# A decode-attention kernel whose loads of K, V and weights go through one ring of 4 MiB contiguous tiles

## The chip, the cores and the metric

The kernel runs on one core of a Trainium2 chip. The metric is device time in microseconds (us), the median of several executions. Before the change it is 2669.64 us (three runs, 2669.05 to 2670.12). Timed experiments come with a 95% interval from fast runs alone. An experiment of a single look has one time beside a run of the kernel before on the same chip; its state is unknown, and I use it only for differences far above 1%, or together with its trace.

## The reference, cut to what matters

```python
x  = A_x                                    # 1 x 1 x 448, bf16
xn = layernorm(x)
q  = (xn @ wq) -> 16 heads x 256            # wq 448 x 4096
scores = q . k_cache * 256**-0.5            # k_cache 16 x 65536 x 256, bf16 (537 MB)
o  = softmax(scores) @ v_cache              # v_cache the same size
s  = o.reshape(4096) @ wo                   # wo 4096 x 448
g  = silu(silu(xn @ w1) @ w2)               # w1 448 x 1792, w2 1792 x 448
out = x + s * g
```

One query token attends to 65536 cached tokens in 16 heads. Every byte of K and V is used once, so the kernel is a reader of 1074 MB with some arithmetic beside it.

One weakness of this reference: s·g is tiny beside x. So the comparison doesn't prove the attention of any kernel here; it is right by construction where the same sums are made.

## The kernel before

K comes in units of 2 MiB (128 partitions x 32 rows of 256). VectorE makes 19 of the 32 dot products of a partition with one fused instruction each, and a wide product for the other 13, which ScalarE sums one by one. (Each fused instruction and each sum stands in before's trace as two, the second reading the total out: 417 and 80 ns on the mean on DVE, 401 and 186 on ACT. So the counts below are about twice those of the loops.)

```python
kp_pool = tc.tile_pool(name="kp", bufs=3);  v_pool = tc.tile_pool(name="vp", bufs=4)
...
Kh = K_t[0, h].rearrange("(j c) d -> j c d", j=P)          # a partition's rows: 256 KiB apart
k_eng.dma_start(out=Kp[:, :, :], in_=Kh[:, kd * KC : (kd + 1) * KC, :])
for i in range(ND):                                          # ND = 19
    nc.vector.tensor_tensor_reduce(out=junk[:, :], in0=Kp[:, i, :], in1=qh, ...,
                                   op0=ALU.mult, op1=ALU.add, accum_out=S_d[:, u, i : i + 1])
nc.vector.tensor_tensor(out=prod[:, :, :], in0=Kp[:, ND:KC, :], in1=qh broadcast, op=ALU.mult)
for i in range(NPU):                                         # NPU = 13
    nc.scalar.activation(out=junk2[:, :], in_=prod[:, i, :], func=ACT.Identity,
                         accum_out=S_a[:, u, i : i + 1])
```

After 8 such units (a block, half a head) a softmax over the block follows. Then TensorE (PE) multiplies the weights with V, 32 matmuls of 256 columns per 2 MiB of V, while the K units of the next block are interleaved. K and V loads share one queue (q1 in the page), issued by SyncE (SP) in the order of the program. wq, w1, w2 and wo are loaded first, and the whole query and the MLP are computed before the first K load, issued at 59.4 us, since the K buffers lie where those weights lay.

## Time and profile before

| what | before |
|---|---|
| time | 2669.64 us |
| DMA, share of its 16 engines' time | over 90% in slices 3 to 39 of 40 |
| VectorE (DVE) busy | 2229.9 us, 84%, 10312 instructions |
| ScalarE (ACT) busy | 1397.5 us, 52%, 6843 instructions |
| PE busy | 1469.9 us, 55%, 8722 matmuls and 8722 weight loads |

The page cuts the span into 40 equal slices; a digit is the busy share in tenths, and the row "GB/s" is what the 16 DMA engines moved together. The prediction shows those rows. A part of the page that it did not show becomes the centre of this case, so here it is, the page's part 3 for before (queue, kind: packets, MB, share of the time of 16 engines):

```profile
q8 instruction: 68, 1.11, 0.2%
q14 instruction: 145, 1.19, 0.1%
```

The page calls their kind "instruction", and their number follows that of the instructions: 10240 more on DVE bring 79 more packets on q14 (e2 below), 17408 more PE records bring 68 on q8 (e3). So I read them as the engines' own programs, fetched while they run. They cost the DMA engines that bring K and V time, as the packet records below show (975 ns for one). The sizes follow from the lines: 1.19 MB / 145 is 8 KiB on q14, 1.11 MB / 68 is 16 KiB on q8, and those packets have 8192 and 16384 B in the trace. The counts of e2 and e3 make 130 instructions to a packet of q14 and 256 to one of q8. With 128, my rounding, DVE's 10312 make 81 and ACT's 6843 make 53 packets, which with about 8 that do not belong to the loops (the experiment e1 below has 8 with almost no instructions) gives 142 of the 145 on q14. PE's 17444 records at 256 to a packet make 68, which is q8. In the share column this is nothing: 0.1% and 0.2%.

### The profile page before, as it was taken

To read this page: it belongs to the slowest core of one execution; us is meant where nothing else is said; L and a number is where in the kernel's file an instruction comes from. 1 tells how busy PE (TensorE), PEld (TensorE's weight loads), DVE (VectorE), ACT (ScalarE), POOL (GpSimd) and SP (SyncE) were. 2 spreads that over 40 slices of the span, in tenths; PEclk is the share of its full clock that TensorE was granted. 3 is DMA by queue.
4 is the path that set the end of the run, shared out by engine and by line. 5 is a ranking of instruction groups with operands and counts; after the bars stand their busy time and mean duration, and the time that the engine had idled before them with its cause. 6 is when DMAs were issued, how large, how long until landed. Compare 5 with 4: busy or idle time off the path is not lost.

```text
span 2669.2 us, 36113 instructions
## 1 busy us (share of the span) xinstructions
PE 1469.9 (55%) x8722; PEld 912.7 (34%) x8722; DVE 2229.9 (84%) x10312; ACT 1397.5 (52%) x6843; POOL 1.6 (0%) x12
## 2 busy tenths in 40 slices
PE   4055655555556565555555555555555565555556
PEld 2033333333333333333333333333333333333334
DVE  1998888888888888888888888888888888888983
ACT  0565555555555555545555554555555555555552
POOL 0000000000000000000000000000000000000000
PEclk9577777777776877777787777677777767776778
DMA  5899999999999999999999999999999999999996
GB/s 197 336 416 427 427 427 427 427 424 414 416 415 419 424 414 412 417 411 417 427 412 419 409 414 422 422 412 417 411 418 426 413 415 413 419 411 425 413 420 279
DMA packets 80919, 1086.63 MB, mean 407 GB/s; under 512 B 8385, under 2 KB 14274, under 8 KB 14722
## 3 DMA queue, kind: packets, MB, share of 16 engines
q1 hardware_dynamic: 74242, 1077.45, 95.9%
q10 hardware_dynamic: 6432, 6.88, 0.8%
q8 instruction: 68, 1.11, 0.2%
q14 instruction: 145, 1.19, 0.1%
q0 software_dynamic: 32, 0.00, 0.0%
HBM read 1084.29 MB, written 0.00 MB: 406 GB/s over the span
## 4 chain that ended last, share of the span: by engine, by line
DMA 48%; DVE 42%; ACT 6%; PE 2%; issue 1%; ACTq 0%; DVEq 0%; SPq 0%
DMA Kp<-in_A_k_cache_dram 46%; DVE junk L258 31%; DVE prod L271 9%; ACT junk L279 6%; DMA Vt<-in_A_v_cache_dram 1%; PE ps_O L426 1%; DMA wo_sb<-in_A_wo_dram 1%; DVE S_d L258 1%; PE ps_q L166 0%; DVE gm L305 0%; DVE rmax_a L298 0%; PE ps_y L216 0%; PE ps_h L203 0%; DVE dlt L357 0%; DVE q_row_bf L188 0%
## 5 line engine op out<-in xcount | busy, mean ns | idle before, releaser
L279 ACT ACTIVATE junk<-prod 128x256 bf16<-128x256 bf16 x3328 | 1330.7, 401 | 1129.2 <-DVE prod L271 1078.8
L258 DVE CUSTOM_DVE_ANT_0 junk<-Kp,qb 128x256 bf16<-128x256 bf16 x4864 | 1709.2, 417 | 251.1 <-DMA Kp<-in_A_k_cache_dram 249.9
L426 PE MATMUL ps_O<-Vt,P_V 128*1 128x256 bf16 x8192 | 1404.0, 353 | 927.0 <-DMA Vt<-in_A_v_cache_dram 927.0
L426 PEld LDWEIGHTS <-P_V 128*1 128x1 bf16 x8192 | 875.8, 107 | 1445.7 <-issue 967.7
L279 ACT ACTIVATION_READ_ACCUMULATOR junk<-prod 128x1 f32 x3328 | 620.6, 186 | 0.0
L271 DVE TENSOR_TENSOR prod<-Kp,qb 128x3328 bf16<-128x3328 bf16 x256 | 482.2, 1884 | 0.0
L258 DVE DVE_READ_ACCUMULATOR2_ANT S_d<- 128x1 f32 x4864 | 387.8, 80 | 0.0
L301 PE MATMUL ps_mrow<-ident_bf,rmax 128*1 128x128 bf16 x32 | 7.9, 247 | 180.4 <-DVE rmax L299 180.4
L301 PEld LDWEIGHTS <-rmax 128*1 128x1 bf16 x32 | 2.5, 79 | 192.4 <-DVE rmax L299 192.4
L298 DVE TENSOR_REDUCE rmax_a<-S_a 128x1 bf16<-128x104 f32 x32 | 8.5, 264 | 59.1 <-ACT junk L279 59.1
L386 DVE SCALAR_TENSOR_TENSOR o_row<-ps_O,cf,o_row 1x256 f32<-1x256 f32 x16 | 7.5, 472 | 60.0 <-PE ps_O L426 60.0
L311 ACT ACTIVATE negb<-ps_nb 128x1 f32<-128x1 f32 x32 | 5.5, 171 | 51.4 <-PE ps_nb L307 51.4
L324 PE MATMUL ps_tot<-ones_col_f,rsum_d 128*1 128x1 f32 x64 | 6.1, 164 | 27.1 <-ACT P_V L315 27.1
L324 PEld LDWEIGHTS ps_tot<-ones_col_f,rsum_d 128*1 128x1 f32 x64 | 2.7, 81 | 43.5 <-ACT P_V L315 43.5
L152 PE MATMUL ps_gen_i<-one_bf,xn_bf 1*128 1x1 bf16 (+1 forms) x4 | 0.4, 178 | 28.0 <-DVE xn_bf L142 28.0
L140 DVE RECIPROCAL rstd<-rstd 1x1 f32<-1x1 f32 x1 | 0.2, 151 | 18.1 <-ACT rstd L137 18.1
L137 ACT ACT_TABLE_LOAD x1 | 1.3, 1283 | 25.6 <-issue 25.6
L396 PE MATMUL ps_ot<-one_f,o_row 1*128 1x1 f32 x64 | 9.6, 251 | 9.0 <-DVE o_row L386 9.0
L315 ACT ACTIVATE P_V<-S_d,negb 128x152 bf16<-128x152 f32 x32 | 13.6, 424 | 1.0
L396 PEld LDWEIGHTS ps_ot<-one_f,o_row 1*128 1x128 f32 x64 | 8.3, 185 | 13.7 <-DVE o_row L386 13.7
L198 ACT CAST qb<-ps_qb 128x512 bf16<-128x512 f32 x5 | 2.9, 586 | 18.6 <-PE ps_qb L191 18.6
L403 DVE CAST OT<-ps_ot 128x2 bf16<-128x2 f32 x16 | 2.6, 160 | 11.1 <-PE ps_ot L396 11.1
(60 smaller groups left out, 167.5 us busy)
## 6 DMA issues: line engine op xcount, KB each, us to landing
Kp<-in_A_k_cache_dram SPq DMA_DIRECT2D x256, 2048.0 KB, 21.7
Vt<-in_A_v_cache_dram SPq DMA_DIRECT2D x256, 2048.0 KB, 26.1
wo_sb<-in_A_wo_dram ACTq DMA_DIRECT2D x1, 3584.0 KB, 23.6
wq_sb<-in_A_wq_dram SPq DMA_DIRECT2D x3, 1024.0 KB, 8.3
w_sb<-in_B_w_dram ACTq DMA_DIRECT2D x1, 1568.0 KB, 8.6
w_sb<-in_B_w_dram ACTq DMA_DIRECT2D x3, 448.0 KB, 8.5
wq_sb<-in_A_wq_dram SPq DMA_DIRECT2D x1, 512.0 KB, 13.9
w_sb<-in_B_w_dram ACTq DMA_DIRECT2D x1, 224.0 KB, 5.3
```

The source lines that it names most:

```text
L198: nc.any.tensor_copy(out=qb[:, g * 512 : (g + 1) * 512], in_=ps_qb[:, :])
L258: nc.vector.tensor_tensor_reduce(out=junk[:, :], in0=Kp[:, i, :], in1=qh, scale=1.0, scalar=0.0, op0=ALU.mult, op1=ALU.add, accum_out=S_d[ ...
L271: nc.vector.tensor_tensor(out=prod[:, :, :], in0=Kp[:, ND:KC, :], in1=qh[:, None, :].to_broadcast([P, NPU, Dh]), op=ALU.mult,)
L279: nc.scalar.activation(out=junk2[:, :], in_=prod[:, i, :], func=ACT.Identity, accum_out=S_a[:, u, i : i + 1],)
L298: nc.vector.reduce_max(out=rmax_a[:, :], in_=S_a[:, :, :], axis=AX.XY)
L301: nc.tensor.matmul(ps_mrow[0:1, :], lhsT=rmax[:, 0:1], rhs=ident_bf[:, :], start=True, stop=True)
L311: nc.scalar.mul(out=negb[:, :], in_=ps_nb[:, :], mul=-scale)
L315: nc.scalar.activation(out=P_V3[:, :, 0:ND], in_=S_d[:, :, :], func=ACT.Exp, bias=negb[:, 0:1], scale=scale, accum_out=rsum_d[:, 0:1],)
L324: nc.tensor.matmul(ps_tot[0:1, 0:1], lhsT=rsum_d[:, 0:1], rhs=ones_col_f[:, 0:1], start=True, stop=(S_a is None),)
L386: nc.vector.scalar_tensor_tensor(out=o_row[0:1, :], in0=ps_O[0:1, :], scalar=cf[0:1, b : b + 1], in1=o_row[0:1, :], op0=ALU.mult, op1=ALU.add,
L396: nc.tensor.matmul(ps_ot[:, n : n + 1], lhsT=o_row[0:1, a * P : (a + 1) * P], rhs=one_f[0:1, 0:1], start=True, stop=True,)
L426: nc.tensor.matmul(ps_O[0:1, :], lhsT=P_V[:, cvl : cvl + 1], rhs=Vt[:, i, :], start=(cvl == 0), stop=(cvl == CPB - 1),)
```

## The change

The intent: keep the DMA engines fed from the first microsecond to the last.

- One ring of five 4 MiB tiles serves wq, K, V and the last weights; every tile is one contiguous stretch of memory, 32 KiB per partition.
- Loads are issued in a fixed order: wq, K, K, then K and V by turns, V a softmax block behind K; w1, w2 and wo come behind the last V.
- The query is computed on all partitions directly, one group of 512 columns at once, so that K work starts after the first group.
- A fixed program order: products ahead of dots, so that ScalarE sums beside DVE; the softmax spread over later half tiles; a block is 16384 tokens.
- V matmuls take two tokens at a time: 512 columns instead of 256.

```diff
-N_DVE_PER_UNIT = 19
-NUM_BLOCKS = 2
+KT = 64
+SUB = 32
+ND = 19
+TPB = 2
+RING = 5
...
+    ring = ctx.enter_context(tc.tile_pool(name="ring", bufs=RING))
+    ctx.enter_context(tc.manual_schedule())
...
+    nc.sync.dma_start(
+        out=wq_t[0:DP, 0 : DC * HD], in_=A_wq.rearrange("(p c) n -> p (c n)", c=DC)
+    )
+    Kh = A_k_cache[0].rearrange("h (t p c) d -> h t p (c d)", p=P, c=KT)
+    Vh = A_v_cache[0].rearrange("h (t p c) d -> h t p (c d)", p=P, c=KT)
...
+    for ki, (h, t) in enumerate(tiles):
+        Kt = load_k(h, t)
+        for s in range(NS):
+            prod = products(h, Kt, s)
+            turn()
+            sums(h, t, s, prod)
+            dots(h, t, Kt, s)
+        if vi < (ki // TPB) * TPB:
+            vh, vt = tiles[vi]
+            attend(vh, vt, load_v(vh, vt))
...
+        if t % TPB == TPB - 1:
+            block_max(h, t // TPB)
+    while vi < len(tiles):
+        vh, vt = tiles[vi]
+        Vt = load_v(vh, vt)
+        if vi == len(tiles) - 1:
+            ... loads of w1, w2 and wo into ring tiles
```

The dots and the sums themselves stay what they were: 19 fused instructions and 13 sums per 32 rows.

## The prediction

> **What bounds the kernel now.** I read the page's slices first, then a table of windows, the queue's own waits, and the chain and timeline of the end. The slices:
>
> ```profile
> PEclk9577777777776877777787777677777767776778
> DVE  1998888888888888888888888888888888888983
> ...
> DMA  5899999999999999999999999999999999999996
> GB/s 197 336 416 427 427 427 427 427 424 414 416 415 419 424 414 412 417 411 417 427 412 419 409 414 422 422 412 417 411 418 426 413 415 413 419 411 425 413 420 279
> ```
>
> The DMA engines are full from slice 3 to slice 39, at 427 GB/s on the best plateau. 1073.7 MB of K and V (16 heads x 65536 x 256 x 2 bytes, twice) must be read whatever the program is. VectorE (DVE) at 8 tenths is second. So the bound is the transfer, and the question is where the 16 engines do not run at 427. The windows answer (columns: window, length, busy of PE, weight load, DVE, ACT, POOL with instruction counts, granted clock, DMA share, GB/s):
>
> ```profile
> 0.00:66.70 66.70, 27.38 (x242) 17.81 (x242) 9.95 (x22) 6.50 (x10) 1.57 (x12) 0.96 0.57 197
> 66.70:133.50 66.80, 0.00 (x0) 0.00 (x0) 66.22 (x312) 37.05 (x182) 0.00 (x0) 0.50 0.83 336
> 200.00:500.00 300.00, 165.34 (x981) 102.67 (x980) 258.84 (x1203) 163.15 (x802) 0.00 (x0) 0.76 1.01 427
> 1000.00:1500.00 500.00, 279.40 (x1629) 172.33 (x1626) 427.73 (x1985) 269.37 (x1326) 0.00 (x0) 0.75 0.99 417
> 2600.00:2640.00 40.00, 25.40 (x167) 16.44 (x166) 22.34 (x98) 17.02 (x84) 0.00 (x0) 0.74 0.76 305
> 2640.00:2670.00 30.00, 22.22 (x197) 16.37 (x194) 1.85 (x4) 0.00 (x0) 0.00 (x0) 0.98 0.59 250
> ```
>
> Time lost against 427 is length x (1 - rate/427). Head (0 to 200 us, with the stretch of 133.5 to 200 at 416): 35.9 + 14.2 + 1.7 = 51.8 us. Middle (200 to 2600; 418, 417, 415 and 416 in the four windows of 500 us, 423 in the last 100): 10.5 + 11.7 + 14.1 + 12.9 + 0.9 = 50.1 us. Tail: 11.4 + 12.4 = 23.8 us. Sum 125.7; and 1086.63 MB / 427 = 2544.8 us, which with 125.7 makes 2670 us. The account closes.
>
> The **head**: the queue has nothing to move while the query and the MLP are computed.
>
> ```profile
> 36.00:40.00 4.00, 3.37 (x40) 2.89 (x39) 1.36 (x3) 0.00 (x0) 0.00 (x0) 1.00 0.00 0
> ...
> SPq L254 <- DVE g_f L225: 25.7, 1, 25.7
> ```
>
> The first K load waits 25.7 us for the gate g_f, since the K buffers lie where the init weights lay. Then three 2 MiB K buffers, with no V allowed before the first softmax, leave the rate at 336 while DVE works.
>
> The **middle**: the queue is in order, and stops where a K buffer is not yet free.
>
> ```profile
> 1008.76 0.33 SPq L254 DMA_DIRECT2D Kp<-in_A_k_cache_dram  x1
> 1009.18 0.38 SPq L423 DMA_DIRECT2D Vt<-in_A_v_cache_dram  x1
> 1022.19 0.33 SPq L254 DMA_DIRECT2D Kp<-in_A_k_cache_dram  x1
> ...
> 1020.00:1024.00 4.00, 2.00 (x19) 1.41 (x17) 3.96 (x16) 1.80 (x9) 0.00 (x0) 1.00 0.57 197
> ...
> DVE rmax_a L298 <- ACT junk L279: 59.1, 30, 5.2
> ```
>
> Loads are normally 8 to 10 us apart, but once per softmax block the gap is 13.4 us: DVE waits for ScalarE's last sums (59.1 us in 30 waits), K comes free late, V stands behind K, and the engines run dry for about 2 us. The early plateau at 427 does not contradict this: the K issues recur at the same 80 to 81 us per block throughout, so the early blocks were living on V transfers queued during the head.
>
> The **tail**: the last K lands at 2614.8; the last V tiles wait for the last softmax and for four V buffers; the last V lands at 2659.9 and 9.3 us of finishing follow.
>
> [...]
>
> **The change part by part.**
>
> *Work on the engines.* DVE's K work is the same per 2 MiB: 19 dots at a pitch of 345 ns (6.56 us) and one product of 1.82 us, 8.4 us. Per 4 MiB tile it is 16.8, and one K plus one V tile take 8.39 MB / 427 = 19.65 us. A block of two tiles is then 33.6 + about 1.5 of softmax = 35 of 39.3 us. The products now come before the dots, so ScalarE's 13 sums (5.3 us) run under the 6.56 us of dots and the rmax_a wait goes. V: 4096 matmuls of 512 columns instead of 8192 of 256, the same streamed columns[...]. PE fits.
>
> *Buffers.* The ring holds five 4 MiB tiles, shared. In steady state K lands at time 0 and is used up by about 20; its slot is next written at 39.3. V lands[...], and is rewritten after 39. V lags by a block: P·V's weights are ready about 21 us after the block's last K lands, while the first V of that block lands 29.5 us after it. A new stall exists: the maximum's small matmul stands in PE's order behind a V tile[...], and slots have 20 us of slack. So the middle loss goes from 50.1 to about 0.
>
> *Head.* wq (3.67 MB) and then K are issued at once; query(0) needs only wq. DVE starts slower than the transfer (K at 21, 31, 41 us; done at 33, 50, 70), and I checked each slot in order: wq's slot is free near 27 and wanted at 51; the first K's at 33, wanted at 60; the third K's at 70, wanted at 80; the fourth K's at 87, wanted at 100. None stalls. Left: 2.3 us before bytes flow (183 GB/s in the first 4 us of before) and about 1.1 us for wq at 380 instead of 427 (the rate of before's weight loads): 3.4 instead of 51.8 us.
>
> *Tail.* MLP and out weights (6.88 MB, about 18.1 us at 380, of which 16.1 are in the byte sum) follow the last V. Work after the last V byte, from before's durations: [...]32 matmuls at 0.22, 7.0; copy of the block 0.7; 16 fp32 turns recorded as 32 at 0.15, 4.8; hidden layer 4.1 (56 recorded in 4.07); silu in four small ops 1.0; ps_y 4 (14 in 4.74[...]); 32 out matmuls of 448 columns 8.5[...]; two 0.61 us ops and a store of 2.4, 3.7. Sum 35.8 us after the last V byte, so 35.8 - 16.1 = 19.7 us are loss (before: 23.8). The tail gains little: the final work moves onto the path while weights load under part of it.
>
> *Sum.* 2544.8 + 3.4 + 0 + 19.7 = 2568. Less about 1 us of instruction fetch (some 8000 fewer PE records of 36113; 2.3 MB of fetch in all)[...]: **2563 us**, 4% less than 2669.6.
>
> **The rivals.** (a) *The transfer itself changes rate.* [...]If the true sustainable rate is about 418 and early 427 was special, 54 us more: 2617. Against it: full windows between dips in the middle still read 426. (b) *DVE becomes the bound* through fixed order: the max wait behind V, or a write conflict on the one score tile that ScalarE and DVE now share (before kept two). [...]If dots had to wait for ScalarE's sums on every half tile, 8.4 + 5.3 = 13.7 us x 256 half tiles = some 3500 us. The instructions write disjoint columns, so I hold this unlikely. (c) *The head is not gained*: a late query or a slot not free in the first blocks; at most 30 us back, 2593. (d) *The tail grows*[...].
>
> **Range and chances.** Most of the gain is arithmetic of idle DMA time seen in the trace: 48 head, 50 middle, 4 tail. Rivals (a), (c), (d) move it by 10 to 40 us. Range 2538 to 2608. The 2% line is 2616; only a full (a) or (b) crosses it. Faster 0.93, same 0.05, slower 0.02.
>
> **What would show it.** Right: GB/s near 427 from slice 1 to 39 with no dips; DVE about as busy (2200 us) but waiting for K and not holding it; queue waits short of starving; the first dot near 16 us; DMA idle only in the last 18 us. Wrong: a DMA share of 1.0 at a rate under 420 (a), DVE without idle time or long waits for ScalarE or PE (b), idle DMA in the first two slices (c).

The sum came to 2563 us, but terms are cut from the text above: 4 us subtracted for longer rows (2544.8 + 3.4 + 0 + 19.7 - 1 - 4 = 2563), and 2 us for a landing, which are still within the 35.8. "PE fits" is left as a guess. What was measured: 32 V matmuls took 3.65 to 6.57 us in before (256 columns, two such groups to 4 MiB) and 7.07 to 10.01 us in after (512 columns, one group to a tile); the 0.22 of the tail is after's (7.07 us for the last 32), not one of before's durations.

## The result, and the profile after

The changed kernel takes **2632.63 us** (2630.22 to 2633.67, four fast runs) against 2669.88 of before in the same rounds: a ratio of 0.986 (0.9846 to 0.9874), 1.4% faster. That is "within 2%", it lies outside my range of 2538 to 2608, and it is 70 us above the prediction. Ratios here are the mean time of one kernel's fast runs over that of the other's of the same rounds, so not quite the ratio of the medians that I quote.

The slices of after:

```profile
DVE  6988888888888888888888888888888888888883
...
DMA  9999999999999999999999999999999999999994
GB/s 377 431 431 429 430 431 430 429 430 431 422 422 410 422 417 415 421 419 421 416 415 422 416 416 414 416 409 410 418 419 418 414 413 425 416 416 418 406 422 171
```

The hole in the head is gone: the first slice reads 377 instead of 197, the second 431 instead of 336. Then 430 holds for nine slices, and from slice 11 the rate sinks to about 416, as it did in before, although the DMA row says that the engines are never short of work. The windows (columns as in the prediction) say the same:

```profile
0.00:66.70 66.70, 18.39 (x54) 6.68 (x55) 45.45 (x203) 34.02 (x144) 1.13 (x11) 0.77 0.98 378
...
200.00:500.00 300.00, 151.62 (x562) 59.22 (x560) 257.33 (x1195) 167.31 (x814) 0.00 (x0) 0.70 1.00 430
...
1000.00:1500.00 500.00, 256.71 (x940) 102.07 (x939) 426.76 (x1981) 274.46 (x1337) 0.00 (x0) 0.71 0.99 418
```

In the four windows of 500 us between 500 and 2500, before has 418, 417, 415, 416 and after has 422, 418, 415, 416. DVE is not what holds it: one line of the table of waits (us in total, times, longest) shows it waiting for K:

```profile
DVE prod L181 <- DMA Kt<-in_A_k_cache_dram: 373.4, 123, 16.6
```

The wait for rmax_a that my prediction blamed is gone, DVE stands idle for K in nearly every tile, and the pace is that of before: in the queue's timeline, 49 consecutive pairs of a K and a V tile between 1012 and 2003 us take 20.22 us each. Before, a pair half as large recurs every 10.1 us.

The end of after tells what kind of limit this is. Four windows of 4 us each:

```profile
2592.00:2596.00 4.00, 4.00 (x14) 1.31 (x13) 0.00 (x0) 0.00 (x0) 0.00 (x0) 0.67 0.72 264
2596.00:2600.00 4.00, 4.00 (x20) 1.55 (x19) 0.00 (x0) 0.00 (x0) 0.00 (x0) 1.00 0.09 36
2600.00:2604.00 4.00, 2.68 (x16) 1.08 (x14) 0.66 (x4) 0.00 (x0) 0.00 (x0) 1.00 0.05 22
2604.00:2608.00 4.00, 4.00 (x20) 1.54 (x19) 0.00 (x0) 0.00 (x0) 0.00 (x0) 1.00 0.06 26
```

Everything, V and the weights behind it, has been issued by now. From 2596 on, the share is 0.05 to 0.09 at 22 to 36 GB/s. One engine of 16 is a share of 0.06, and a sixteenth of 430 is 27 GB/s: **one single DMA engine** still works. The last V tile landed only at 2601.6 us, as PE's timeline shows (start, length, and in brackets the idle time before and what ended it):

```profile
2601.57 7.07 PE L261 MATMUL psO<-Vt,PV 128*2 128x512 bf16 x32 [1.32 <-DMA Vt<-in_A_v_cache_dram]
2608.57 4.47 PE L318 MATMUL ps_ot<-cf,O 2*128 2x1 f32 x32
2612.97 3.52 PE L411 MATMUL ps_h<-xnT,w 112*128 112x1 bf16 x56
2617.52 4.97 PE L430 MATMUL ps_y<-w,h1s 128*1 128x448 bf16 x14 [1.03 <-DVE h1s L424]
2622.33 6.22 PE L443 MATMUL ps_ao<-wo,OT 128*1 128x448 bf16 x32
```

In before, the last V came at 2659.9 and 9.3 us followed. In after it comes 58.3 us earlier and 30.3 us follow, 21 more: that is the whole gain of 37 us.

Which engine lags, and why? Part 3 of after's page is almost that of before:

```profile
q1 hardware_dynamic: 39490, 1084.31, 98.0%
q14 instruction: 141, 1.16, 0.1%
q8 instruction: 38, 0.62, 0.1%
```

The trace also holds every packet, with start, size, queue and length (though not the number of the DMA engine). Around one fetch in after they read (on the packets' own clock, which starts some 10 us before the page's):

```
192419 ns    8192 B  q14  took  333 ns
192740 ns   32768 B  q1   took 1875 ns
```

A data packet of 32 KiB otherwise takes 1213 ns. The one behind such a fetch takes 1875 ns and most often starts 313 ns after it (321 here), so fetch and packet together take 2188 ns instead of 1213: **975 ns lost** on that DMA engine. In before it is the same 975 ns (1586 against 611 for its 16 KiB packets). A second kind of 8 KiB fetch costs 687 ns.

That gives **theory A**, to be tested. DVE's fetches all travel on one DMA engine. Its 80 fetches of 975 ns make it 78 us late over the kernel. A tile is complete only when all 16 engines have brought their sixteenth (the last V landed at 2601.6, after some 5 us with one engine at work), so the kernel ends with the laggard. The 15 others run ahead until the ring's slots are used up, which is the early plateau of 430, and from then on move at the laggard's pace. ACT's 54 fetches of 687 ns are 37 us on another engine and hide behind DVE's. A change that leaves the number of DVE instructions (10221 instead of 10312) leaves the middle.

**Rivals**: (B) the memory or the bus gives no more than 416 in the long run, or slows after some time; (C) the layout or the length of rows; (D) PE's work or its fetches; (E) too little slack in the ring, so a deeper one would help.

### The profile page after: what moved, and what is told of

Read it like the earlier page. It is cut to its first block, busy times and chain, and to the rows that moved or that the text cites. A ratio compares the mean times of both kernels' runs of the same rounds, so it can differ in the third digit from the quotient of the medians.

```text
span 2631.8 us, 27942 instructions
## 1 busy us (share of the span) xinstructions
PE 1323.3 (50%) x4906; PEld 520.5 (20%) x4906; DVE 2204.1 (84%) x10221; ACT 1431.0 (54%) x6941; POOL 1.1 (0%) x11
## 4 chain that ended last, share of the span: by engine, by line
DMA 68%; DVE 16%; PE 13%; ACT 3%; issue 0%; SPq 0%; DVEq 0%
DMA Kt<-in_A_k_cache_dram 45%; DMA Vt<-in_A_v_cache_dram 23%; DVE junk_d L207 11%; PE psO L261 10%; DVE prod L181 4%; ACT junk_a L194 2%; PE ps_ot L318 2%; DVE S L207 0%; PE ps_ao L443 0%; ACT PV L243 0%; ACT O L272 0%; PE ps_y L430 0%; PE ps_h L411 0%; DVE gmax L235 0%; ACT neg L241 0%
## 5 line engine op out<-in xcount | busy, mean ns | idle before, releaser
L194 ACT ACTIVATE junk_a<-prod 128x256 bf16<-128x256 bf16 x3328 | 1329.4, 400 | 694.5 <-DVE prod L181 480.7
L207 DVE CUSTOM_DVE_ANT_0 junk_d<-Kt,qb 128x256 bf16<-128x256 bf16 x4864 | 1698.4, 411 | 0.0
L261 PE MATMUL psO<-Vt,PV 128*2 128x512 bf16 x4096 | 1179.0, 459 | 1002.9 <-DMA Vt<-in_A_v_cache_dram 1000.8
L181 DVE TENSOR_TENSOR prod<-Kt,qb 128x3328 bf16<-128x3328 bf16 x256 | 482.6, 1885 | 373.5 <-DMA Kt<-in_A_k_cache_dram 373.4
L261 PEld LDWEIGHTS <-PV 128*2 128x2 bf16 x4096 | 395.4, 97 | 1848.4 <-issue 1392.3
L194 ACT ACTIVATION_READ_ACCUMULATOR junk_a<-prod 128x1 f32 x3328 | 620.2, 186 | 0.0
L207 DVE DVE_READ_ACCUMULATOR2_ANT S<- 128x1 f32 x4864 | 359.9, 74 | 0.0
L318 PE MATMUL ps_ot<-cf,O 2*128 2x1 f32 x512 | 103.2, 327 | 66.1 <-ACT O L272 66.1
L318 PEld LDWEIGHTS ps_ot<-cf,O 2*128 2x128 f32 x512 | 100.9, 295 | 112.1 <-ACT O L272 67.4
L237 PE MATMUL ps_nb<-gmax,ones_row_bf 1*128 1x1 bf16 x64 | 10.1, 159 | 174.9 <-DVE gmax L235 174.9
L272 ACT COPY O<-psO 2x512 f32<-2x512 f32 x64 | 35.7, 557 | 18.2 <-PE psO L261 18.2
```

The source lines that it names most:

```text
L181: nc.vector.tensor_tensor(out=prod[:, :, :], in0=Kt[:, s * SUB + ND : (s + 1) * SUB, :], in1=q[:, None, :].to_broadcast([P, NA, Dh]), op=A ...
L194: nc.scalar.activation(out=junk[:, :], in_=prod[:, i, :], func=ACT.Identity, accum_out=S[:, at + i : at + i + 1],)
L207: nc.vector.tensor_tensor_reduce(out=junk[:, :], in0=Kt[:, s * SUB + i, :], in1=q, scale=1.0, scalar=0.0, op0=ALU.mult, op1=ALU.add, accum ...
L261: nc.tensor.matmul(st["psO"][:, :], lhsT=st["PV"][:, i0 * KT + 2 * i : i0 * KT + 2 * i + 2], rhs=Vt[:, i * 2 * Dh : (i + 1) * 2 * Dh], sta ...
L272: nc.scalar.copy(out=O[:, :], in_=st["psO"][:, :])
L318: nc.tensor.matmul(ps_ot[:, n : n + 1], lhsT=Ov[:, j, a, :], rhs=cf[:, b, j : j + 1], start=(b == 0 and j == 0), stop=(b == NB - 1 and j = ...
```

## The experiments

Twelve kernels ran. Before was run beside them, with medians of 2670.26 to 2670.38.

### e1: only the loads

```diff
-            prod = products(h, Kt, s)
-            turn()
-            sums(h, t, s, prod)
-            dots(h, t, Kt, s)
+        touch(Kt)          # nc.vector.tensor_copy of one column, to free the slot
```

V tiles are touched likewise; the attention's result OT is set to zero.

> The changed kernel's loads in the same order through the same ring, with one one-column DVE copy per tile in place of all attention work; the result is wrong on purpose. Theory A (one of the 16 DMA engines also carries the instruction fetch of a busy engine, falls behind by 0.97 us for each 8 KiB fetch of DVE and 1.55 us for each 16 KiB fetch of PE, and every tile waits for it): almost no instructions, so no laggard; a K and V pair every 19.4 us to the end, about 2519 us. Rival B (the memory itself delivers 416 instead of 430 GB/s after the first 700 us): a pair every 20.2 us, about 2610 us. Rival C (DVE frees the slots too late): also about 2519 us.

2543.15 us. Its page:

```profile
PE 24.5 (1%) x138; PEld 11.9 (0%) x138; DVE 47.8 (2%) x270; ACT 8.3 (0%) x13; POOL 1.1 (0%) x11
...
GB/s 380 432 433 431 432 432 431 432 432 431 432 433 431 431 433 431 431 433 431 431 433 431 431 433 431 431 433 432 431 433 432 431 432 433 430 433 431 432 433 281
...
q14 instruction: 8, 0.07, 0.0%
```

The same loads in the same order through the same ring hold 432 to the end. So (B) falls: the memory sustains 432. The time is 24 us above what I expected. A pair of tiles takes 19.45 us, not 19.36, which over 128 pairs is 11 us; the rest lies in the head and the tail, which I didn't take apart.

### e2, e12, e3, e10: instructions put back, one engine at a time

Each adds idle instructions per K tile to e1; they touch nothing that the loads need.

```diff
     def extra():
-        pass
+        for _ in range(80):                    # e2; 40 in e12
+            nc.vector.memset(scrap[:, :], 0.0)
+        # e3:  68 matmuls  ps_x <- ident_bf[:, 0:2], ident_bf[:, 0:2]
+        # e10: 80 times    nc.scalar.copy(out=scrap[:, :], in_=ident_bf[:, 0:1])
```

> The loads alone, plus 80 one-column DVE writes per K tile: DVE's instruction count comes back (about 10,500), its busy time does not. Theory A: about 84 more DVE fetches x 0.975 us on one DMA engine, about 82 us more than the loads alone, 2600 us, a pair every 20.1 us. Rivals B and C: no change against the loads alone.

> The loads alone plus 40 one-column DVE writes per K tile, half the dose of the earlier run (80 gave 79 us more). Theory A: 42 more fetches x 0.975 us = 41 us more than 2543, about 2583 us, the ring's lead used up about twice as late. Anything that steps rather than grows in proportion speaks against it.

> The loads alone, plus 68 two-column matmuls per K tile: the 17,400 PE instructions of the kernel before, with next to no PE time. Theory A: about 68 fetches of 16 KiB x 1.55 us, about 105 us more than the loads alone, 2624 us. If PE's fetch does not weigh on one DMA engine: no change.

> The loads alone plus 80 one-column ScalarE copies per K tile, 10,240 in all. If ScalarE's 8 KiB fetches sit on one DMA engine too: 80 fetches x 0.685 us = 55 us more than the loads alone (2543), 2598. If they are spread like PE's: 2547.

| run | added | fetches added | time (one look) | above e1 | expected above e1 |
|---|---|---|---|---|---|
| e2 | 10240 on DVE | 79 on q14 | 2621.93 | +79 | +82 |
| e12 | 5120 on DVE | 39 on q14 | 2577.32 | +34 | +41 |
| e10 | 10240 on ACT | 80 on q14 | 2591.62 | +48 | +55 |
| e3 | 8704 matmuls and as many weight loads on PE | 68 on q8 | 2555.26 | +12 | +105 |

e2 is the decisive one. DVE is busy for 641 of 2622 us, with an instruction that waits for the loads only once per tile, and still the loads take 79 us longer, one microsecond per fetch. Its page:

```profile
GB/s 381 431 432 431 431 431 431 432 430 431 431 431 430 432 430 431 430 416 416 415 424 415 417 419 413 416 420 412 419 416 414 415 418 418 411 416 418 417 418 120
...
q14 instruction: 87, 0.71, 0.1%
```

The shape is that of after: a plateau, then a step to 416. If a fetch stalled all 16 engines, the rate would be low from the start. If fetches were spread over them, 79 x 0.975 us would be shared and make 5 us. Only a lone laggard with a lead to use up gives a late step and the whole 79 us. Half the instructions (e12) give a little under half the time, and the plateau lasts about twice as long:

```profile
GB/s 382 431 431 432 431 431 431 432 431 432 431 432 431 432 431 432 431 432 431 432 431 432 432 432 431 431 432 432 431 431 432 432 431 421 425 421 425 425 421 118
```

The packets of these traces say it directly. A packet most often starts 3 to 4 ns before another one ends. I take two such packets as neighbours on one DMA engine and join packets into 16 chains, one per engine (where two engines run in step the joining can slip). In e12, 15 chains have moved their last byte by 2534.9 us of the packets' clock and the sixteenth at 2569.6. In e2 it is 2580.6 and 2614.3. Followed back from its last packet of 32 KiB, that late chain carries DVE's last fetch in e2 and DVE's last three in e12. So the laggard is the engine with the fetches. Why the DMA row stays at 9 while 15 engines wait for one shows here too: e2's packets of 32 KiB take 1219 ns on the mean before the step and 1242 to 1253 behind it, so their share of the time stays near 1.0 while they move less. A full share is not a full rate.

e3 is a **miss of mine**: I took PE's fetches to sit on one engine too, and expected 2624. They cost 12 us. PE runs ahead of the loads there, so 68 of the 69 fetches fell in the first 480 us, and the rate in that stretch is 427 to 430 instead of 432, from the second slice on, with no late step:

```profile
GB/s 380 428 427 428 430 427 428 430 431 433 432 432 432 432 432 431 433 431 433 432 431 433 431 433 431 431 433 431 432 431 432 432 431 433 430 432 432 431 432 243
...
q8 instruction: 69, 1.13, 0.2%
```

So PE's fetches are spread. The chains say over how many: the eighth fetch after a given one is on the same chain in 45 of 60 cases, the next one in 2 of 67, so they go round 8 of the 16 engines. A PE fetch costs its engine 1.55 us in these packets; 68 of them over 8 engines are 13 us each, and 12 were measured. With e7 and e8 below, (D) falls.

e10 says that ACT's, like DVE's, sit on one engine: 48 us for 80 fetches, 0.60 us each, somewhat below the 0.687 of the packet records. Here too there is a late step:

```profile
GB/s 381 429 432 432 429 432 432 430 432 431 431 432 431 432 432 432 430 433 431 430 433 432 430 430 417 423 422 422 420 418 420 424 416 421 423 417 427 431 434 123
```

The step's place can be worked out too. The laggard loses (fetches per pair of tiles) x (loss per fetch) each 19.5 us, and the others can be ahead by so many tiles as the ring allows. A tile of 4 MiB is 128 packets of 32 KiB, so a sixteenth of it is 8 packets, at 1213 ns each 9.7 us. The falls are read from slices of about 65 us:

| run | lost per pair | rate falls at | lag by then | in tiles |
|---|---|---|---|---|
| e2 | 0.61 us (DVE) | about 1115 us | 35 us | 3.6 |
| e12 | 0.30 us (DVE) | about 2125 us | 33 us | 3.4 |
| e10 | 0.46 us (ACT, a fetch each 28.8 us) | about 1555 us | 37 us | 3.8 |
| after, ring 5 | 0.61 us (DVE) | about 660 us | 21 us | 2.1 |
| e6, ring 4 | 0.61 us (DVE) | about 330 to 390 us | 10 to 12 us | 1.1 to 1.3 |

Where slots are free at once (e2, e12, e10), about the same lag (33 to 37 us) ends the plateau, whatever it took to build up; it is also how late the last chain ends in e2 and e12. Where slots are held by the dots, the lead is smaller, and one tile less in the ring is one tile less of lead.

### e6: a ring of four

```diff
-RING = 5
+RING = 4
```

> The changed kernel with a ring of four tiles instead of five. Theory A: the ring only sets how far the 15 fast engines can run ahead of the slow one; the pair still takes 20.1 to 20.2 us, the time is 2632 to 2642 us, and the rate falls from 430 to 416 near 350 us instead of near 650, since the lead is about one tile (10 us) shorter. Rival C (buffers and the order of the queue hold the middle back): a longer pair, over 2660 us.

2634.66 us (2632.32 to 2636.01), ratio to before 0.9865 (0.9851 to 0.988). No slower than after, to within the runs, and the plateau ends earlier, as expected:

```profile
GB/s 381 430 428 431 429 425 419 413 416 413 422 419 409 418 419 415 417 421 420 413 421 416 418 412 418 418 417 411 414 426 415 413 420 418 415 418 416 416 414 230
```

(E) falls: the depth of the ring decides how long the others can run ahead, not when the laggard arrives. The early plateau is borrowed time.

### e5: rows 256 KiB apart, as before had them

```diff
-    Kh = A_k_cache[0].rearrange("h (t p c) d -> h t p (c d)", p=P, c=KT)
+    Kh = A_k_cache[0].rearrange("h (p t c) d -> h t p (c d)", p=P, c=KT)
     (V likewise)
```

> The changed kernel with the contiguity of the tiles undone: the same 32 KiB runs, but 256 KiB apart from partition to partition, as the kernel before has them. Theory A (DVE's fetches on one DMA engine set the pace of the middle): the same time, 2632 +- 8 us. If contiguous tiles are worth something: slower, by up to the 4% between 432 and 416 GB/s.

2636.76 us (2631.21 to 2636.82), ratio 0.9869 (0.9854 to 0.9884) against 0.986 of after. (C) falls as far as contiguity goes: nothing beyond the noise, the two intervals overlap. The length of a row is worth something: a packet of 16 KiB takes 611 ns in before and one of 32 KiB 1213 ns in after, 9 ns less than two short ones. Over the 2047 long packets of each engine (32752 in after's trace, by 16) that is about 18 us, too little for (C), and e1 against after, with equal rows, leaves it no part in the step.

### e7: twice the matmuls in the real kernel

```diff
             nc.tensor.matmul(st["psO"][:, :], ...)
+            nc.tensor.matmul(
+                ps_ao[0:1, 0:2], lhsT=ident_bf[:, 0:1], rhs=ident_bf[:, 0:2], start=True, stop=True
+            )
```

> The changed kernel with a two-column matmul added behind each V matmul: 8192 more PE instructions with next to no time, so PE has the 68 to 76 fetches of the kernel before. If PE's 16 KiB fetches are spread over the 16 DMA engines, as the loads with PE instructions suggest (12 us for 69): at most 8 us more, 2640. If they sit on one engine: 70 x 1.55 = 109 us beats DVE's 92, about 2650 us.

2633.53 us (2630.71 to 2634.8), ratio 0.986. PE now fetches 70 packets instead of 38, about what before had, and nothing changes. So the halved number of V matmuls, a part of this change, is worth nothing here as far as instructions and their fetches go.

### e4 and e8: the same dots in fewer instructions

In e4, 17 dots per 32 rows are made by two wide products and two reductions (15 go to ACT). In e8, 26 dots are made by one wide product, two in-place halving additions and one reduction, and 6 are left to ACT:

```diff
-ND = 19
+ND = 26
...
-        for i in range(ND):
-            nc.vector.tensor_tensor_reduce(... accum_out=S[:, at + i : at + i + 1])
+        nc.vector.tensor_tensor(out=pd[:, :, :], in0=Kt[:, s * SUB : s * SUB + ND, :],
+                                in1=q broadcast, op=ALU.mult)
+        for n in (Dh // 2, Dh // 4):
+            nc.vector.tensor_tensor(
+                out=pd[:, :, 0:n], in0=pd[:, :, 0:n], in1=pd[:, :, n : 2 * n], op=ALU.add
+            )
+        nc.vector.tensor_reduce(
+            out=S[:, at : at + ND], in_=pd[:, :, 0 : Dh // 4], axis=AX.X, op=ALU.add
+        )
```

> The changed kernel with its 19 two-instruction dots per half tile replaced by two products and two reductions over 17 columns (ScalarE sums 15): a right result, DVE down from about 10,200 to about 1,800 instructions at about the same busy time[...]. Theory A: DVE's fetches go, and the engine with PE's 38 fetches x 1.55 = 59 us is the next laggard instead of 92 us: about 2600 us. Rivals B and C: 2632 us, or slower where DVE is the bound.

> The changed kernel with DVE's dots replaced by wide instructions: one product of 26 columns, two halving additions and one reduction per half tile, and ScalarE sums only 6 columns. DVE about 1,500 and ScalarE about 3,400 instructions instead of 10,200 and 6,900. Theory A: neither fetch stream weighs; a pair about 19.6 us, 2565 to 2575 us, against 2588 for the wide version whose ScalarE still had 7,965 instructions and 2632 for the changed kernel. If what was left in the wide version was DVE's load (95% busy): no better than 2588.

e4: 2588.81 us (2588.38 to 2590.07), ratio 0.9694 (0.9678 to 0.971). DVE has 1517 instructions, ACT 7965, so now ACT's engine is the laggard: 62 fetches of 0.687 us are 43 us, against 78 of DVE before, a gain of 35 us by this account; measured 44. (I had expected 2600, with PE's fetches as the next laggard, which e3 refuted; and the 92 us that I gave DVE's engine there and in e7 should have been 78.)

e8: **2566.03 us** (2565.4 to 2566.4), ratio 0.9609 (0.9595 to 0.9623). It beats both kernels, after by 67 us. Its page:

```profile
PE 1311.7 (51%) x4906; PEld 513.9 (20%) x4906; DVE 2414.1 (94%) x1517; ACT 717.6 (28%) x3357; POOL 1.1 (0%) x11
...
GB/s 376 431 431 428 432 431 430 430 432 430 429 431 433 429 431 431 431 430 431 431 430 431 431 431 430 431 432 429 431 432 430 430 432 431 430 432 432 429 431 185
...
q14 instruction: 45, 0.37, 0.0%
```

DVE is *busier* than in after, 2414 against 2204 us, and the kernel is faster, since DVE was not the bound. What fell is its number of instructions: 1517 of DVE make 12 fetches (12 us), 3357 of ACT make 26 (18 us). The step at slice 11 is gone. By theory A the gain is 78 - 18 = 60 us; 67 were measured. This also answers a rival that I had not listed, that the engines' own traffic slows the loads: DVE works more here than in after, and the loads hold 431.

Both kernels write the products, and e8 two additions as well, into bf16 tiles (e8's trace: prod_d, 128x6656 and 128x3328 bf16), where the fused instruction's total goes to an fp32 tile (after's trace: S, 128x1 f32). The attention is the same sum by construction, but I take it to be a little coarser; by how much is not shown, as the comparison can't tell. A user would have to check that against a real tolerance.

### e9: the same rewrite in the kernel before

```diff
-N_DVE_PER_UNIT = 19
+N_DVE_PER_UNIT = 26
     (dots by one wide product, two halvings and one reduction, as in e8)
```

> The kernel before, untouched but for its dots: the wide product, two halving additions and one reduction over 26 columns, ScalarE summing 6. Theory A (the kernel before was held by DVE's fetches on one DMA engine as well): a head's K and V take about 157 instead of 161.5 us, the time is 2590 to 2605 us. Rival D (the prediction's reading: the dips once per softmax block, from waits of the in-order queue, cost the middle 50 us and are a loss of their own): the dips stay, 2640 us or more.

2615.16 us (2614.66 to 2616.73), ratio 0.9794 (0.9779 to 0.9808). The slices:

```profile
GB/s 205 331 394 428 428 428 428 428 427 428 428 428 427 427 428 427 428 427 427 429 428 428 427 427 428 428 427 428 428 428 428 427 427 427 426 428 428 427 427 302
```

It is 10 us above the top of what I expected, but the shape is clear. The middle is flat at 428: before's dips, which I had laid to the softmax and the in-order queue, vanish while the softmax, the queue and the buffers are what they were. The head and the tail are about what they were (the third slice is lower, 394 against 416). But e9 takes away one thing more: with 6 sums instead of 13 on ScalarE, the wait rmax_a <- ACT junk (59.1 us in before) is gone from its waits as well. So e9 alone doesn't tell the two causes apart. After does: it lost that wait and kept the loss. And the packets of before fit the laggard: between 1030 and 1034 us of their clock, in one dip, the number of DMA engines at work falls from 16 to 1 and not to 0; from 500 to 2500 us of e9 it is never below 12. So before had the same laggard; whether the wait made its dips deeper is not tested.

### e11: the out weights and the MLP first

```diff
-RING = 5
+RING = 4        # wo is held outside the ring
     query(0)
+    (loads of w1, w2, wo and the whole MLP moved here from the end)
```

> The changed kernel with the part 'out weights last' undone: w1, w2 and wo loaded and the MLP computed before K, wo kept resident, ring of four tiles to make room. Against the ring of four (2634.7): K starts 16 us later; after the last V 30.3 us of tail become about 22. So about 8 us slower, 2640 to 2645, if hiding the weights' transfer under the last work is worth what the sum says; equal or faster if the work on the MLP in the tail costs as much as it hides.

2641.25 us (2639.82 to 2645.76), ratio 0.9888 (0.9872 to 0.9905). Against the ring of four with the weights last (2634.66), putting them last is worth about 7 us.

## Why the prediction was wrong

**The middle: the step that failed.** The prediction says "So the middle loss goes from 50.1 to about 0". It stayed: the four windows of 500 us lose 57 us against 430, where before's lost 49 against 427. The premise was that the dips came from K buffers held for ScalarE's last sums. That wait did vanish, as predicted (DVE waits 373.4 us for K), and the rate did not follow. e9 shows the other half: with DVE's instructions cut and the softmax as it was, before's dips go. By theory A the dips were how the laggard showed: a K tile late by one engine, and behind it 15 engines out of loads.

**The term that was mis-sized.** "Less about 1 us of instruction fetch" counted 2.3 MB of fetch over 16 engines. What DVE's cost is not their bytes but 975 ns each, and they do not spread: 78 us on DVE's engine, by e2 79 us for 10240 instructions. I read the share column of part 3 (0.1%) as an upper limit of the cost. It is a mean over 16 engines, and the kernel waits for the slowest.

**The early plateau.** I saw early slices at 427 in before as a sign of the true rate with stalls later, fed by "V transfers queued during the head". The rate was true (e1 holds it), but the plateau was 15 engines running ahead. e6 shows it, by ending it sooner without a loss of time.

**The rivals.** Rival (a), "If the true sustainable rate is about 418 and early 427 was special", had the right symptom, a share of 1.0 at under 420, and the nearest number, 2617. Its cause, the transfer itself, is refuted by e1. I argued against it that full windows between dips still read 426; in before's packets all 16 engines have work there, which a laggard allows as well. Rivals (b), (c) and (d) did not come: DVE has slack, the rate is 430 from 66.7 to 133.5 us, so that no late slot shows, and the tail is shorter than I had it.

**The head: right mechanism.** Two lines of the timeline of after:

```profile
18.44 6.54 PE L138 MATMUL ps_q<-wq,xnT 112*128 112x512 bf16 x16 [12.61 <-DMA wq<-in_A_wq_dram]
...
23.16 1.89 DVE L181 TENSOR_TENSOR prod<-Kt,qb 128x3328 bf16<-128x3328 bf16 x1 [16.59 <-DMA Kt<-in_A_k_cache_dram]
```

DVE's K work starts at 23.2 us, where before made its first dot at 67.3 us; I had said near 16. wq landed at 18.4 rather than about 12 us, which 2.3 us and 3.67 MB at 380 make: in the first 20 us the engines moved only 197 to 324 GB/s at a share of 0.77 to 1.04, which I didn't take apart. The first 66.7 us at 378 lose 66.7 x (1 - 378/431) = 8.2 us, where I had 3.4. Of before's 51.8 us in the head some 44 are won, as intended; with the 16 us of weights moved to the end this makes 60, and the last V does come 58.3 us earlier.

**The tail: about right.** I had 33.8 us after the landing of the last V; it is 30.3. (The recorded 35.8 held 2 us more for the landing, the term cut above: in before's trace the last V lands 0.3 us after its last packet has ended.) But the weights that should have filled this time had landed before it for 15 engines of 16, so the tail is almost pure idle time.

**The sum.** It said 2563, and e8, the change with few DVE instructions, measures 2566. That is closer than the terms deserve, and partly luck: e8 still has about 18 us of lag by this account and the head lost 5 us more than I had, while the tail was 3.5 us shorter and the longer rows saved about 18 us, where the term cut above was 4.

**What stays open.** The number of the DMA engine that carries the fetches of DVE or of ACT, and why PE's spread, the trace can't say. Why a data packet behind a fetch takes 662 ns longer is not known. A pair in after takes 20.22 us, where 19.45 + 0.61 makes 20.06; a burst of slow packets as 15 engines restart together may be the 0.16, but that is argued, not tested. e12 and e10 cost 4 to 7 us less than their fetches add up to. A fetch doesn't cost the same throughout: after the step, the mean in e2's packets is 0.85 to 0.91 us, so that 79 us for 79 fetches is a near match and not a constant. And the precision of the attention in e4, e8 and e9 is not proved by the comparison.

## What to carry to other kernels

When a load-bound kernel moves fewer bytes per second than the same loads alone, count instructions, not only busy time: put the loads by themselves, then add idle instructions one engine at a time. In this stream of large tiles, fewer and wider VectorE and ScalarE instructions paid even where they kept the engine busier: e8 is 67 us faster than after with DVE busy for 2414 us instead of 2204. And a high rate at the start that sinks later (431 to about 416 GB/s here), at a DMA share of 0.99 to 1.00, asks for a look at the last microseconds: in after, a share of 0.05 to 0.09 there, about one sixteenth, was the sign of a lone laggard.
